# Seven experts of a mixture-of-experts layer, selected by one switch each instead of nested branches

## The chip, the core and the metric

The kernel runs on one core of a Trainium2 chip. A core has five engines with instruction streams of their own: TensorE (PE in the profile; its weight loads are listed as PEld), VectorE (DVE), ScalarE (ACT), GpSimd (POOL) and SyncE (SP), and 16 DMA engines that move data between memory and the core. The metric is device time in microseconds (us) of one execution; smaller is better.

## The reference

A block-sparse attention is followed by a mixture of experts in which some tokens skip the experts:

```python
def _attn_ref(q, k, v, sampled_blocks):      # B=4, H=8, S=768, D=64, blocks of 32
    scores = scale * np.matmul(q, k.transpose(0, 1, 3, 2))
    # kept: blocks next to each other, first and last block row and column, 3 sampled blocks a row
    scores = np.where(mask, scores, -1000000000.0)
    attn = softmax(scores)
    return np.matmul(attn, v)

def _moe_ref(x, w_skip, w_gate, w1, w2):     # x: 3072 tokens of 512; 8 experts, 1024 inner columns
    out = x.copy()
    xc = x[x @ w_skip > 0]
    e_idx = np.argmax(xc @ w_gate, axis=1)
    gate_w = softmax(xc @ w_gate)[row, e_idx]
    for e in range(E):
        h = np.maximum(xc[e_idx == e] @ w1[e], 0.0)
        y[e_idx == e] = gate_w[...] * (h @ w2[e])
    out[x @ w_skip > 0] = xc + y
    return out
```

How many tokens an expert gets is known only while the kernel runs. With these inputs the largest of the eight comes first; the sizes, in groups of 32 tokens, are 12 for expert 0 and then 8, 10, 9, 5, 2, 10 and 11 for experts 1 to 7, in the order in which the kernel works them off.

## The kernel before

The attention comes first (up to about 310 us): batch by batch, with the routing of finished tokens between its steps. It is not changed. The experts follow. Products are made in a split form: an operand is held as a high and a low part (`h` and `l` in the names), and each product is three matmuls, high by high, high by low, low by high.

Expert 0 has a branch of its own (`ahead`), in which counting, sorting and the first gathers stand between its matmuls. `counts()` makes `cnt`, the number of groups of 32 tokens of each expert, on VectorE; the sorted list `lt` follows it there, and GpSimd's gathers of token rows read that list.

Experts 1 to 7 stand one after the other in the program, each with the code for every size that it might have:

- `gemm1_any(n, e, x, each)` chooses a width by nested `tc.If` (lines 782 to 803) and calls `gemm1` (lines 746 to 754), 96 matmuls of 256 to 384 columns into PSUM tiles `hp`, which ScalarE and VectorE read as they come (`hh`, `hf`, `hl`); at most four groups go through `gemm1_tokens` (lines 768 to 778) instead.
- `outputs(p, n)` goes through the second product in chunks of 128 tokens. `last_chunk` (lines 898 to 914) does the last one first: whole (`gemm2`, lines 812 to 814), or, if it has only 64 or 32 tokens, by `gemm2_few` (line 824), chosen by two more compares; which chunk is the last is chosen by another two. In it the next expert's rows are turned (`turn`, line 588, PSUM tiles `tp` and `rps`). `full_chunks` (lines 934 and 938) does the others.
- Around these, weights are loaded two experts ahead (`load_w`, line 488: first weights on SyncE's queue, second ones on GpSimd's) and split into the two parts (`split_w`, lines 492 and 494). `close` (line 829) writes a chunk out, and `fetch_rows` (line 576) gathers rows for two experts ahead on GpSimd.

Each engine has its own instruction stream, and every engine runs every compare. An `If` of the program thus stands as compares and jumps in all five streams, and in each the code of the branches not taken lies between what is executed. The number `n` that the compares use is read by `tokens_of`:

```python
    n = tokens_of(1)
    for e in range(1, E):
        gemm1_any(n, e, x, parts(e))
        n = outputs(e, n)
```

The PSUM tiles come from pools: two tiles for turned rows (`ps_x`), three for the first product (`ps_h`), two for the second (`ps_y`), and the rest for the routing.

Of the kernel before, what the change touches and what calls it, by code (L numbers as in the profile page):

```python
# [30 lines left out]
CS = 3  # L31
# [3 lines left out]
NEVER = float(E * LC * P * P)  # L35
VA = 8
NEAR = 8
BATCHES = [[0, NB - 1, 1, 2], [3, 4, 5, 6], [7, 8, 9, 10], [11, 12, 13, 14], [15, 16, 17], [18, 19, 20], [21, 22]]


@with_exitstack
def tile_kernel(ctx, tc, qs, qd, kt, v, sb, wg, w1, w2, out):
# [548 lines left out]
    def keep_x(tps, xh, xl):  # L591
        for c, tp in enumerate(tps):
            cs = slice(P * c, P * c + P)
            nc.scalar.copy(out=xh[:, :, cs], in_=tp)
            nc.vector.tensor_tensor(out=xl[:, :, cs], in0=tp, in1=xh[:, :, cs].bitcast(F32), op=ALU.subtract)
# [115 lines left out]
    wp2 = ctx.enter_context(tc.tile_pool(name="wp2", bufs=1))  # L711
    mp = ctx.enter_context(tc.tile_pool(name="mp", bufs=2))
    mc = ctx.enter_context(tc.tile_pool(name="mc", bufs=1))
    ps_x = ctx.enter_context(tc.tile_pool(name="ps_x", bufs=2, space=PSUM))
    ps_h = ctx.enter_context(tc.tile_pool(name="ps_h", bufs=3, space=PSUM))
    ps_y = ctx.enter_context(tc.tile_pool(name="ps_y", bufs=2, space=PSUM))
    cnt = mc.tile([1, E], I32, name="cnt")
    mxc = mc.tile([1, 1], I32, name="mxc")
    one = mc.tile([1, 1], I32, name="one")
    lt = mc.tile([P, E * LC, 2], I32, name="lt")  # L720
    ends = mc.tile([P, CS, 2], I32, name="ends")
    lsw = mc.tile([P, LC, 2], I32, name="lsw")
# [113 lines left out]
    def counts():  # L836

        c = count("c")
        nc.vector.tensor_scalar(out=cnt, in0=c, scalar1=float(G - 1), scalar2=None, op0=ALU.add)
        nc.vector.tensor_single_scalar(out=cnt, in_=cnt, scalar=5, op=ALU.logical_shift_right)  # L840
        nc.vector.tensor_reduce(out=mxc, in_=cnt, axis=AX.X, op=ALU.max)
        er = nc.vector.value_load(perm[0:1, 0:1], min_val=0, max_val=E - 1)
        nc.vector.tensor_copy(out=one, in_=cnt[:, bass.ds(er, 1)])
        nc.vector.tensor_copy(out=cnt[:, bass.ds(er, 1)], in_=cnt[:, 0:1])
        nc.vector.tensor_copy(out=cnt[:, 0:1], in_=one)

    def lists():
        nc.sync.dma_start(out=lt, in_=lst3)
# [9 lines left out]
            gather(xs[p % 2][c], lt[:, p * LC + c, 0:1])  # L858

    def columns(xgs, x):  # L860
        keep_x(turn_x(xgs[:2], ps_x, "tp") + turn_x(xgs[2:], ps_r, "rps"), *x)

    def parts(p):

# [80 lines left out]
    def tokens_of(p):  # L945
        return nc.values_load(cnt[0:1, p:p + 1], min_val=0, max_val=N // G)

    def outputs(p, n):

        def split_next(zs):  # L950
            if p + 1 < E:
                for z in zs:
                    split_w("1", p + 1, z, 8, "hl", nc.gpsimd if z in (7,) else None)

        def turn():
            if p + 1 < E:
                columns(xs[(p + 1) % 2], x)

        last_chunk(p, n, lambda: split_next((0, 1)), turn)
        if p + 2 < E:  # L960
            load_w("1", p + 2)
        split_next(range(2, NEAR))
        nxt = tokens_of(p + 1) if 0 < p < E - 1 else None
        full_chunks(p, n)
        if p + 2 < E:
            load_w("2", p + 2, eng=nc.gpsimd)
        return nxt

    wt.update({"2" + t: wp2.tile([P, 4096], F32R, name=f"w2{t}") for t in "hl"})
    xs = [[mp.tile([P, DM], F32, name=f"x{z}{c}", bufs=1) for c in range(CS)] for z in range(2)]  # L970
# [7 lines left out]
    with tc.If(pv > 1) as ahead:  # L978
        px, p0, p1, d1, d2, rank, d3, d4 = last[0]()
        le = early["l"]  # L980
        load_w("2", 1, 0, 2)

        beside = [[px], [], [p0], [p1, d1], [d2], [], [], [rank, d3], [], [d4], [], [counts, lists, lambda: load_w("2", 1, 1, 2)]]
        splits = [[], [], [], [0], [1, 2], [3, 4], [5, 6], [7]]

        def go(n):
            for step in beside[n] if n < len(beside) else []:
                step() if callable(step) else run(step)

        for f in range(NK2):  # L990
            gemm1(0, early["t"], 256, None, [f], between=lambda: go(2 * f))
            go(2 * f + 1)
            for z in splits[f]:
                split_w("2", 0, z, 8)
        gemm2(0, 0, 0)
        order_lists()
        rows(0, [2])
        rows(1, range(CS))
        finish(0, early["x"][0], le.bitcast(F32)[:, 0, 1:2], le[:, 0, 0:1])
        clear()  # L1000
        gemm2(0, 1, 1, range(0, 6))
        keep_x(turn_x(xs[0][2:], ps_x, "tp"), *early["t"])
        gemm2(0, 1, 1, range(6, NK2))
        finish(1, early["x"][1], le.bitcast(F32)[:, 1, 1:2], le[:, 1, 0:1])
        n0 = tokens_of(0)
        with tc.If(n0 > 2 * CG):
            gemm1_tokens(0, early["t"])
        columns(xs[1], x)
        for z in range(NEAR):
            split_w("1", 1, z, 8)  # L1010
        load_w("1", 2)
        with tc.If(n0 > 2 * CG):
            gemm2(0, 0, 0)
            close(0, 2, 0, xs[0][2])
        rows(2, range(CS))
        load_w("2", 2, eng=nc.gpsimd)
# [13 lines left out]
        outputs(0, n0)  # L1030
    for z in range(2):
        nc.vector.tensor_scalar(out=ends[:, :, z], in0=lt[:, (E - 1) * LC:(E - 1) * LC + CS, 0], scalar1=2.0, scalar2=float(z), op0=ALU.mult, op1=ALU.add)
    n = tokens_of(1)
    for e in range(1, E):
        gemm1_any(n, e, x, parts(e))
        n = outputs(e, n)


    top = nc.values_load(mxc, min_val=0, max_val=N // G)
# [67 lines left out]
```

## Time and profile before

| what | value |
|---|---|
| time, median of 3 runs | 601.09 us (596.47 to 601.2) |
| the profiled execution | 606.04 us, its span 604.3 us |
| mean granted clock of TensorE | 0.925 |
| busy: TensorE, VectorE, ScalarE, GpSimd | 513.6, 369.8, 251.8, 216.6 us |
| experts 1 to 7 on TensorE | 361.9 to about 591 us |
| instruction transfers, queues q8 and q14 | 88 and 73 packets, 1.44 and 0.60 MB |

The profile is one execution. The chain of waits is followed back from the last instruction. A row of the timeline gives the start, the duration, engine, line, operation and tiles of an instruction (or of several alike, x4), and in brackets how long its engine was idle before it and what ended that, where "issue" stands for nothing that the profile shows. Branches and compares are not counted as busy and have no rows of their own. The granted clock is a share of full speed; 0.50 is half. A row of the DMA view gives a queue's packets, megabytes and share of the 16 engines in the window asked for; q8 and q14 carry instructions.

### The profile page before, as it was taken

To read this page: it belongs to the slowest core of one execution; us is meant where nothing else is said; L and a number is where in the kernel's file an instruction comes from. 1 tells how busy PE (TensorE), PEld (TensorE's weight loads), DVE (VectorE), ACT (ScalarE), POOL (GpSimd) and SP (SyncE) were. 2 spreads that over 40 slices of the span, in tenths; PEclk is the share of its full clock that TensorE was granted. 3 is DMA by queue.
4 is the path that set the end of the run, shared out by engine and by line. 5 is a ranking of instruction groups with operands and counts; after the bars stand their busy time and mean duration, and the time that the engine had idled before them with its cause. 6 is when DMAs were issued, how large, how long until landed. Compare 5 with 4: busy or idle time off the path is not lost.

```text
span 604.3 us, 16232 instructions
## 1 busy us (share of the span) xinstructions
PE 513.6 (85%) x5842; PEld 382.3 (63%) x5842; DVE 369.8 (61%) x1019; ACT 251.8 (42%) x576; POOL 216.6 (36%) x236
## 2 busy tenths in 40 slices
PE   7999999899898899996979768896887958859991
PEld 4777665466565465563668558694776946737981
DVE  4877578478577777787776066544466572735510
ACT  3444455355364355462733055343153535423500
POOL 2016363564655355646372321300404040602011
PEclk9999999799899699897988898987899888979997
DMA  9999899688799499788894415441625454630000
GB/s 295 342 299 236 190 259 243 153 219 211 174 215 232 115 227 224 167 229 214 247 322 142 172 27 179 172 180 24 218 108 178 152 189 158 214 125 26 19 33 22
DMA packets 49507, 108.03 MB, mean 179 GB/s; under 512 B 7175, under 2 KB 35208, under 8 KB 43842
## 3 DMA queue, kind: packets, MB, share of 16 engines
q1 hardware_dynamic: 43760, 84.69, 51.3%
q0 software_dynamic: 5008, 20.69, 9.7%
q8 instruction: 88, 1.44, 1.0%
q14 instruction: 73, 0.60, 0.3%
q10 hardware_dynamic: 578, 0.61, 0.3%
HBM read 96.34 MB, written 12.30 MB: 180 GB/s over the span
## 4 chain that ended last, share of the span: by engine, by line
PE 34%; issue 28%; DMA 21%; DVE 8%; POOL 3%; SPq 2%; POOLq 1%; ACT 0%; ACTq 0%; DVEq 0%
PE sp L400 11%; PE op L434 7%; PE tp L420 6%; DMA kts<-w 5%; DMA out<-o,lt 5%; DMA x<-out,lt 4%; DMA lst<-pay,adr 4%; PE op L356 4%; PE sp L321 3%; DVE m L409 3%; DVE m L408 3%; PE tp L344 2%; DMA out<-xs 2%; POOL out L72 1%; DVE xs L447 1%
## 5 line engine op out<-in xcount | busy, mean ns | idle before, releaser
L400 PE MATMUL sp<-kg,q 128*64 128x256 f32 x704 | 102.0, 408 | 2.8 <-issue 2.7
L424 ACT COPY pt<-tp 128x512 f32<-128x512 f32 x88 | 51.7, 588 | 108.1 <-PE tp L420 96.7
L408 DVE TENSOR_REDUCE m<-sp 128x2 f32<-128x512 f32 x88 | 60.2, 684 | 43.3 <-PE sp L400 35.5
L72 POOL DMA_INDIRECT out<-o,lt x17 | 19.4, 1139 | 179.2 <-DVE o L829 178.9
L201 POOL TENSOR_TENSOR kg<-kts,onesf 128x512 f32<-128x512 f32 x66 | 82.0, 1273 | 0.0
L415 ACT ACTIVATE pr<-sp,m 128x256 f32<-128x256 f32 x176 | 74.4, 478 | 8.0 <-DVE rs L445 8.0
L746 PE MATMUL hp<-xh,w1h 128*128 128x256 f32 (+3 forms) x192 | 61.3, 319 | 16.7 <-issue 8.3
L186 POOL TENSOR_SCALAR kg<-kts 128x512 f32<-128x512 f32 x50 | 30.1, 627 | 125.5 <-PE sp L400 87.4
L400 PEld LDWEIGHTS sp<-kg,q 128*64 128x64 f32 x704 | 45.2, 141 | 36.5 <-issue 24.5
L420 PE MATMUL tp<-ident,pr 128*128 128x128 f32 x352 | 61.8, 297 | 4.4 <-issue 4.4
L434 PEld LDWEIGHTS op<-va,pt 128*32 128x32 f32 x1376 | 31.9, 112 | 47.3 <-ACT pt L424 24.9
L747 PE MATMUL hp<-xl,w1h 128*128 128x256 f32 (+3 forms) x192 | 60.6, 316 | 0.0
L748 PE MATMUL hp<-xh,w1l 128*128 128x256 f32 (+3 forms) x192 | 60.5, 315 | 0.0
L751 ACT ACTIVATE hh<-hp 128x256 fp32r<-128x256 f32 (+2 forms) x56 | 21.2, 381 | 93.6 <-PE hp L748 51.6
L434 PE MATMUL op<-va,pt 128*32 128x65 f32 x1376 | 49.5, 232 | 11.3 <-DVE xs L447 8.5
L434 PE MATMUL op<-vb,pt 128*32 128x65 f32 x1376 | 50.6, 227 | 3.1 <-issue 2.9
L754 DVE SCALAR_TENSOR_TENSOR hl<-hp,hh 128x256 fp32r<-128x256 f32 (+2 forms) x56 | 23.4, 419 | 46.8 <-ACT hf L753 28.4
L746 PEld LDWEIGHTS hp<-xh,w1h 128*128 128x128 f32 x192 | 39.1, 204 | 19.1 <-issue 19.1
L420 PEld LDWEIGHTS tp<-ident,pr 128*128 128x128 f32 x352 | 38.9, 145 | 14.2 <-issue 6.9
L812 PE MATMUL yp<-w2h,hh 128*128 128x512 f32 x112 | 45.0, 402 | 2.7 <-ACT w1h L492 1.6
L813 PE MATMUL yp<-w2l,hh 128*128 128x512 f32 x112 | 44.1, 394 | 0.3 <-DVE o L829 0.3
L814 PE MATMUL yp<-w2h,hl 128*128 128x512 f32 x112 | 44.2, 394 | 0.0
(207 smaller groups left out, 1013.2 us busy)
## 6 DMA issues: line engine op xcount, KB each, us to landing
vb<-v SPq DMA_DIRECT2D x68, 260.0 KB
va<-v SPq DMA_DIRECT2D x48, 260.0 KB
kts<-w SPq DMA_DIRECT2D x6, 2048.0 KB
kts<-w POOLq DMA_DIRECT2D x6, 2048.0 KB
q<-qs SPq DMA_DIRECT2D x22, 512.0 KB
vt<-v SPq DMA_DIRECT2D x16, 390.0 KB
kts<-w SPq DMA_DIRECT2D x12, 512.0 KB
kts<-kt SPq DMA_DIRECT2D x15, 384.0 KB
```

The source lines that it names most:

```text
L201: nc.gpsimd.tensor_tensor(out=kg[x][:, :, c0:c0 + BS], in0=kts[:, :, bass.ds(kr * BS, BS)], in1=onesf[:, 0:BS].unsqueeze(1).broadcast_to([ ...
L400: nc.tensor.matmul(out=self.sp[64 * j:64 * j + 64, g, :], lhsT=qt[self.i][:, p, :], rhs=kg[self.x][:, p, :], start=True, stop=True)
L408: lambda: nc.vector.reduce_max(out=self.mx, in_=self.sp, axis=AX.X),
L415: nc.scalar.activation(out=self.pr[:, g, :], in_=self.sp[:, g, :], func=AF.Exp, bias=self.mx[:, g:g + 1], scale=SCALE)
L420: nc.tensor.transpose(out=self.tp[:, u, :], in_=self.pr[:, u // 2, (u % 2) * P:(u % 2) * P + P], identity=ident)
L424: nc.scalar.copy(out=self.pt, in_=self.tp)
L434: nc.tensor.matmul(out=self.op[32 * hh:32 * hh + 32, g, :], lhsT=self.pt[:, 2 * g + t, 32 * hh:32 * hh + 32], rhs=vt[:, 8 * self.b + 4 * g ...
L746: nc.tensor.matmul(out=hp[:, 0:w], lhsT=wh[:, f, k, :], rhs=xh[:, k, 0:w], start=(k == 0), stop=False)
L747: nc.tensor.matmul(out=hp[:, 0:w], lhsT=wh[:, f, k, :], rhs=xl[:, k, 0:w], start=False, stop=False)
L748: nc.tensor.matmul(out=hp[:, 0:w], lhsT=wl[:, f, k, :], rhs=xh[:, k, 0:w], start=False, stop=(k == NK1 - 1))
L812: nc.tensor.matmul(out=yp, lhsT=hh[:, f, cs], rhs=wh[:, f, :], start=(f == 0), stop=False)
L814: nc.tensor.matmul(out=yp, lhsT=hl[:, f, cs], rhs=wh[:, f, :], start=False, stop=(f == NK2 - 1))
```

## The change

One `tc.Switch` per expert takes the place of all compares between the first product and the end of the second. It has ten arms, for n = 1, 2, 4, 5, 6, 8, 9, 10, 11 and 12 groups (`KINDS`); each arm is a whole expert, `expert(p, n)`, written with n as a constant, so that nothing in an arm branches. Sizes between two kinds take the next larger arm.

- `counts()` makes `kinds` on VectorE: for each expert the number of kinds that `cnt` exceeds, one instruction and then eight more. `kind_of` reads an entry, one expert ahead.
- The PSUM pools `ps_x` (2) and `ps_h` (3) become one pool `ps_h` of five; turned rows take `hp` tiles from it. In expert 0's branch, too, they do.
- The gathers for the chunks from the last one upwards now stand together behind the last chunk. For five groups `gemm1` writes 160 columns, where the old code wrote 192; the matmuls are 256 wide in both.

```diff
-    ps_x = ctx.enter_context(tc.tile_pool(name="ps_x", bufs=2, space=PSUM))
-    ps_h = ctx.enter_context(tc.tile_pool(name="ps_h", bufs=3, space=PSUM))
+    ps_h = ctx.enter_context(tc.tile_pool(name="ps_h", bufs=5, space=PSUM))
...
         nc.vector.tensor_copy(out=cnt[:, 0:1], in_=one)
+        nc.vector.tensor_scalar(out=kinds, in0=cnt, scalar1=float(KINDS[0]), scalar2=None, op0=ALU.is_gt)
+        for n in KINDS[1:-1]:
+            nc.vector.scalar_tensor_tensor(out=kinds, in0=cnt, scalar=float(n), in1=kinds, op0=ALU.is_gt, op1=ALU.add)
...
     def columns(xgs, x):
-        keep_x(turn_x(xgs[:2], ps_x, "tp") + turn_x(xgs[2:], ps_r, "rps"), *x)
+        keep_x(turn_x(xgs[:2], ps_h, "hp") + turn_x(xgs[2:], ps_r, "rps"), *x)
...
+    def kind_of(p):
+        return nc.values_load(kinds[0:1, p:p + 1], min_val=0, max_val=len(KINDS) - 1)
+
+    def expert(p, n):
+
+        if n > CG:
+            gemm1(p, x, G * n, parts(p), few=G * (n % CG) if n % CG < 3 else 0)
+        else:
+            gemm1_tokens(p, x)
+            if n > 2:
+                for f in range(NK2):
+                    split_w("2", p, f, 8)
...
+        c = (n - 1) // CG
+        if c == 0:
+            turn()
+        split_next((0, 1))
+        m = G * (n - CG * c)
+        if m > 64:
+            gemm2(p, c, 1)
+            close(p, c, 1, xs[p % 2][c])
+        else:
+            gemm2_few(p, c, m, 1)
+            close(p, c, 1, xs[p % 2][c], m)
+        if c:
+            turn()
+        for y in range(c, CS):
+            fetch_rows(p + 2, y)
+        if p + 2 < E:
+            load_w("1", p + 2)
+        split_next(range(2, NEAR))
+        for y in range(c):
+            if p == E - 1 and y == c - 1:
+                halves(p, y, y)
+            else:
+                gemm2(p, y, y)
+                close(p, y, y, xs[p % 2][y])
+                fetch_rows(p + 2, y)
+        if p + 2 < E:
+            load_w("2", p + 2, eng=nc.gpsimd)
...
-    n = tokens_of(1)
+    nxt = kind_of(1)
     for e in range(1, E):
-        gemm1_any(n, e, x, parts(e))
-        n = outputs(e, n)
+        kind, nxt = nxt, kind_of(e + 1) if e + 1 < E else None
+        for z in tc.Switch(kind, len(KINDS), hint=f"expert{e}"):
+            expert(e, KINDS[z])
```

Three places show how instructions move. The rows are in the order of the program, with the code of all branches or arms; `hp`, `yp` are PSUM tiles of the first and the second product, `kts` the loaded weights, `w2h` and `w2l` their split parts.

First TensorE's stream where expert 1 ends and expert 2 begins, before:

```order
L814 MATMUL yp_6625<-w2h,hl 128x512
L938 UNCONDITIONAL_BRANCH x2
L782 COMPARE_AND_BRANCH
L783 COMPARE_AND_BRANCH
L784 COMPARE_AND_BRANCH
L746 MATMUL hp<-xh,w1h 128x384
```

and after:

```order
L815 MATMUL yp_6624<-w2h,hl 128x512
L1148 UNCONDITIONAL_BRANCH
L972 TENSOR_LOAD kinds
L1148 SWITCH_STRIDE
L1148 ISA x2
L1088 BRANCH_PREFETCH_HINT
L769 MATMUL hp<-w1h,xh 128x512
```

The three compares ahead of the first matmul are gone (three or four are executed, by size); in their place stand the read of the table, a register operation and an indirect jump (the two rows marked ISA). The hint that opens each arm names the place at which the arm will leave the switch.

Second, TensorE's stream around the last chunk of expert 2 when that chunk is the third, before:

```order
L814 MATMUL yp_6626<-w2h,hl 128x512
L898 UNCONDITIONAL_BRANCH
L902 COMPARE_AND_BRANCH
L824 MATMUL yp_6626<-kts,hf 64x512 x8
L902 UNCONDITIONAL_BRANCH
L824 MATMUL yp_6626<-kts,hf 32x512 x8
L902 UNCONDITIONAL_BRANCH
L588 MATMUL tp<-ident,x_6614 128x128 x4
```

and after, in the arm for ten groups:

```order
L749 MATMUL hp<-xh,w1l 128x320
L825 MATMUL yp_6624<-kts,hf 64x512 x8
L589 MATMUL hp<-ident,x_6612 128x128 x4
L589 MATMUL hp<-ident,x_6613 128x128 x4
L589 MATMUL rps<-ident,x_6614 128x128 x4
L813 MATMUL yp_6623<-w2h,hh 128x512
```

The few-row products follow the first product directly, and the next expert's rows are turned into `hp` tiles.

Third, VectorE's stream in expert 0's branch, where the counts are made, before:

```order
L843 COPY one<-cnt 1x1
L844 ISA
L844 COPY cnt<-cnt 1x1
L845 COPY cnt<-one 1x1
L494 TENSOR_TENSOR w2l<-kts,w2h 128x512 x2
```

and after:

```order
L845 ISA
L845 COPY cnt<-cnt 1x1
L846 COPY cnt<-one 1x1
L847 TENSOR_SCALAR kinds<-cnt 1x8
L849 SCALAR_TENSOR_TENSOR kinds<-cnt,kinds 1x8 x8
L495 TENSOR_TENSOR w2l<-kts,w2h 128x512 x2
```

Nine instructions on 8 numbers stand ahead of the rest of the second weights' split and of the sorted list.

More of the change, by code (lines that the diff above doesn't have):

```diff
@@ L37 @@
 NEAR = 8
+KINDS = [1, 2, 4, 5, 6, 8, 9, 10, 11, 12]
 BATCHES = [[0, NB - 1, 1, 2], [3, 4, 5, 6], [7, 8, 9, 10], [11, 12, 13, 14], [15, 16, 17], [18, 19, 20], [21, 22]]
@@ L719, in tile_kernel @@
     one = mc.tile([1, 1], I32, name="one")
+    kinds = mc.tile([1, E], I32, name="kinds")
     lt = mc.tile([P, E * LC, 2], I32, name="lt")
@@ L962, in outputs @@
         split_next(range(2, NEAR))
-        nxt = tokens_of(p + 1) if 0 < p < E - 1 else None
         full_chunks(p, n)
@@ L966, in outputs, with split_next, turn @@
             load_w("2", p + 2, eng=nc.gpsimd)
-        return nxt
+    def kind_of(p):
[8 more added lines that the diff above has]
+                    split_w("2", p, f, 8)
+        def split_next(zs):
+            if p + 1 < E:
+                for z in zs:
+                    split_w("1", p + 1, z, 8, "hl", nc.gpsimd if z in (7,) else None)
+        def turn():
+            if p + 1 < E:
+                columns(xs[(p + 1) % 2], x)
+        c = (n - 1) // CG
[25 more added lines that the diff above has]
+            load_w("2", p + 2, eng=nc.gpsimd)
     wt.update({"2" + t: wp2.tile([P, 4096], F32R, name=f"w2{t}") for t in "hl"})
@@ L1001, in tile_kernel @@
         gemm2(0, 1, 1, range(0, 6))
-        keep_x(turn_x(xs[0][2:], ps_x, "tp"), *early["t"])
+        keep_x(turn_x(xs[0][2:], ps_h, "hp"), *early["t"])
         gemm2(0, 1, 1, range(6, NK2))
```

## The prediction

> **What bounds the kernel now.** I read the page first: the shares of the engines and the chain that ended last.
>
> ```profile
> span 604.3 us, 16232 instructions
> PE 513.6 (85%) x5842; PEld 382.3 (63%) x5842; DVE 369.8 (61%) x1019; ACT 251.8 (42%) x576; POOL 216.6 (36%) x236
> PE 34%; issue 28%; DMA 21%; DVE 8%; POOL 3%; SPq 2%; POOLq 1%; ACT 0%; ACTq 0%; DVEq 0%
> ```
>
> TensorE is busy 85% of the time, but 28% of the chain is "issue": the engine waits for nothing that the profile shows. The change touches experts 1 to 7, which TensorE works on from 361.9 us to about 591 us. The busy time by stretch, here for that whole part and for experts 2, 5 and 7 (columns: window, its length, busy TensorE, weight loads, VectorE, ScalarE, GpSimd, then the granted clock, the DMA share and GB/s):
>
> ```profile
> 355.00:592.00 237.00, 193.23 (x1079) 165.64 (x1077) 122.65 (x193) 84.44 (x203) 52.45 (x48) 0.91 0.36 128
> 390.00:431.00 41.00, 33.50 (x170) 28.32 (x171) 19.15 (x31) 13.76 (x35) 9.40 (x9) 0.88 0.42 153
> 491.00:515.00 24.00, 14.63 (x60) 10.43 (x60) 8.68 (x14) 8.51 (x17) 4.44 (x5) 0.79 0.41 143
> 554.00:592.00 38.00, 36.19 (x209) 33.22 (x207) 12.73 (x21) 7.76 (x16) 4.88 (x5) 1.00 0.09 32
> ```
>
> TensorE is idle 44 of 237 us; VectorE works 123 of them and DMA is busy 36%, so neither can be the limit over the stage. Expert 7, the last, shows what an undisturbed one looks like: 36 of 38 us busy at full clock. The waits of TensorE from 355 to 592 us (total, times, longest) put names to the idle time:
>
> ```profile
> PE yp L824 <- issue: 11.7, 2, 7.1
> PE hp L746 <- issue: 8.3, 3, 3.1
> PE hp L768 <- issue: 7.3, 1, 7.3
> PE hp L746 <- DVE ends L1032: 5.3, 1, 5.3
> PE hp L746 <- DVE w1l L494: 3.0, 1, 3.0
> PE yp L824 <- DVE w2l L494: 2.0, 1, 2.0
> PE yp L812 <- ACT w1h L492: 1.6, 1, 1.6
> PE yp L824 <- ACT w1h L492: 1.5, 1, 1.5
> PE yp L812 <- DVE hl L754: 1.1, 1, 1.1
> ```
>
> Together 41.8 us. Every one stands where the program branches: L746 and L768 open the first product of an expert, behind the compares of `gemm1_any`; L824 and L812 open the last chunk, behind those of `last_chunk`. The timeline gives the places (start, duration, operation, in brackets the idle time before):
>
> ```profile
> 392.87 0.39 PE L746 MATMUL hp<-xh,w1h 128*128 128x320 f32 x1 [3.06 <-issue]
> 413.36 2.79 PE L824 MATMUL yp<-kts,hf 128*64 128x512 f32 x5 [4.63 <-issue]
> 434.03 0.37 PE L746 MATMUL hp<-xh,w1h 128*128 128x288 f32 x1 [2.36 <-issue]
> 468.29 0.36 PE L746 MATMUL hp<-xh,w1h 128*128 128x256 f32 x1 [2.89 <-issue]
> 497.78 0.77 PE L768 MATMUL hp<-w1h,xh 128*128 128x512 f32 x1 [7.30 <-issue]
> 539.25 3.77 PE L824 MATMUL yp<-kts,hf 128*64 128x512 f32 x8 [7.10 <-issue]
> ```
>
> What is waited for in such a gap the DMA view tells. First the queue of instruction transfers in 532.0 to 539.2 us, the gap ahead of the 7.10; then the same queue in 427.8 to 428.2 us; last, TensorE from 427.90 to 431.60 us:
>
> ```profile
> q8 instruction: 2, 0.03, 2.0%
> ...
> q8 instruction: 1, 0.02, 13.9%
> ...
> 427.90:431.60 3.70, 3.70 (x17) 2.81 (x15) 0.00 (x0) 0.00 (x0) 2.04 (x2) 1.00 0.40 125
> ```
>
> Two fetches of 16 KB of instructions fill the idle 7.10 us, at most 3.55 us each. The third row says what hides a fetch: the one at 428 us, for expert 3's entry, began 3.7 us before TensorE ran out of matmuls. The idle time there was 2.36, so two fetches in series took 3.7 + 2.36 = 6.1 us, 3.0 each. A hop thus costs 3.0 to 3.55 us; one alone hides behind the queued 512-wide products, two in a row do not.
>
> The idle time has a second price, the clock. Stretches at half clock after the gaps, and one after the 3.01 us gap that kept full clock:
>
> ```profile
> 360.00:366.60 6.60, 4.73 (x22) 4.76 (x23) 1.57 (x4) 0.89 (x2) 3.66 (x4) 0.50 0.71 186
> 393.97:397.35 3.38, 3.38 (x15) 3.38 (x14) 1.12 (x2) 1.00 (x3) 0.57 (x1) 0.50 0.82 246
> 414.00:417.80 3.80, 3.80 (x11) 1.82 (x9) 0.00 (x0) 0.00 (x0) 0.00 (x0) 0.50 0.00 0
> 434.95:438.30 3.35, 3.35 (x16) 3.35 (x16) 1.10 (x2) 0.98 (x3) 0.72 (x2) 0.50 0.69 187
> 469.10:472.40 3.30, 3.30 (x18) 3.30 (x17) 0.98 (x2) 0.90 (x3) 0.32 (x1) 0.50 0.70 194
> 492.90:503.10 10.20, 5.32 (x13) 4.24 (x14) 2.23 (x4) 0.00 (x0) 2.70 (x4) 0.50 0.54 163
> 537.35:544.10 6.75, 4.85 (x12) 2.17 (x14) 0.00 (x0) 0.00 (x0) 0.00 (x0) 0.50 0.02 5
> 517.90:524.00 6.10, 6.10 (x42) 6.10 (x43) 5.01 (x7) 2.62 (x9) 5.61 (x4) 1.00 0.77 307
> ```
>
> Work at half clock takes twice its time, so half of the busy 28.7 us in the first seven rows, 14.4 us, is lost. Idle and clock together: 56.2 us.
>
> **The change part by part.** *Branches inside an expert.* An arm holds the whole expert as straight code, so the waits ahead of L824 and L812 go: 11.7 + 2.0 + 1.6 + 1.5 + 1.1 = 17.9 us. Some bear an operand's name (w1h, w2l, hl), not "issue"; I take them for fetches too, since the operands named were made on engines that run the same compares.
>
> *Branches at an entry.* Expert 1's 5.3 follows the code ahead of the loop and stays. The others are 8.3 + 7.3 + 3.0 = 18.6 us now, with none at expert 7. In place of three or four compares stand one read of the table of kinds and one indirect jump. The way out of an arm is announced at its start by a hint; the way in is not, so one hop remains, 3.0 to 3.55 us against the 3.7 that run ahead: 0 if it hides, about 3 if the run-ahead is lost (the lone gaps of 2.4 to 3.1). No row prices the table read. I take 1 us for each of experts 2, 3, 4, 6 and 7, nearer to zero because the run-ahead was measured. Expert 5's 7.30 fell among weight loads and was two hops: (7.30 + 3.7) / 2 = 5.5 for one, 1.8 beyond the run-ahead, with the table read 2.5. Entries after: 5 + 2.5 = 7.5, a gain of 11.1 us.
>
> *Clock.* With gaps of 1 us, the half-clock rows at 393.97, 414.00, 434.95, 469.10 and 537.35 go: (3.38 + 3.80 + 3.35 + 3.30 + 4.85) / 2 = 9.3 us. Those at 360 and 492.9 I leave. The rows do not give a sure bound: gaps of 2.36 were followed by half clock, the one of 3.01 was not. [...]
>
> *The table of kinds.* `counts()` gets nine small VectorE instructions. The rows, with the work behind them and the chain they stand in:
>
> ```profile
> 323.11 0.14 DVE L839 TENSOR_SCALAR cnt<-rps 1x8 int32<-1x8 f32 x1
> 323.29 0.16 DVE L840 TENSOR_SCALAR cnt<-cnt 1x8 int32<-1x8 int32 x1
> 324.65 0.14 DVE L845 COPY cnt<-one 1x1 int32<-1x1 int32 x1
> 329.82 1.04 POOL L576 DMA_INDIRECT x<-out,lt  x1 [5.82 <-DVE lt L854]
> 339.16 0.34 PE L588 MATMUL tp<-ident,x 128*128 128x128 f32 x1 [4.14 <-DMA x<-out,lt]
> ```
>
> From start to start 0.18 us, so 9 x 0.18 = 1.6 us. Behind them VectorE still owes the sorted list `lt`, on which GpSimd's gather waits, and on the gather TensorE (4.14 us). Between 0, if the gather's landing is set elsewhere, and 1.6; I take 1.0. The instructions are added on that path, so a gain is excluded.
>
> *Five PSUM tiles.* No wait in the list above names `hp` or `tp` as not free, so five shared tiles gain 0. A turned row now takes a tile of the first product; it comes after that product was read, in expert 5 right behind it, where a sixth tile waits for the first one's reader: 0 to the 1.5 us that the last chunk there waits for ScalarE now (L824, w1h), taken 0.
>
> *Order of gathers, 160 instead of 192 columns.* In a two-chunk expert one gather, in expert 5 three, now come ahead of GpSimd's share of the next split: 1.04 us each, so 1 to 3 us late for a slice that is the last of eight to be used. Taken 0, at most 3 if that slice ends last. The number of matmuls stays. In expert 4 ScalarE and VectorE read 32 columns less in eight tiles, off the path: 0.
>
> Sum: 17.9 + 11.1 + 9.3 - 1.0 = 37.3 us. The profiled execution took 606.04 us (span 604.3, the rest around it) and would take 568.7; it lies 5 us above the median of 601.09, so from the median 563.8, **564 us**.
>
> **The rivals.** *Operands end last.* Once the fetches are gone the waits named w1h, w2l, hl and w1l stay, because VectorE and ScalarE are late themselves: 2.0 + 1.6 + 1.5 + 1.1 + 3.0 = 9.2 us less gain, of which 1 for expert 6's entry is already counted: 8, 572 us. For it speaks the row at 517.90, with VectorE busy 5.01 of 6.10 us; against it 123 of 237 over the stage.
>
> *One hop uncovered at every entry.* The sequencer reaches the jump too late: six entries at 3 us are 18, so of 18.6 only 0.6 is gained; of the clock only the mid-expert stretches, (3.80 + 4.85) / 2 = 4.3, less 0.8 for a new one now and then at expert 7. 17.9 + 0.6 + 4.3 - 0.8 - 1.0 = 21.0: 580 us. For it: the lone entry gaps of 2.36 to 3.06; against it: two hops, not one, explain that of 2.36.
>
> *Two hops in series per expert.* An arm is longer than one block of code, so the jump out is fetched as well as the jump in. Five entries at 3.2 and expert 5 at 7.3 make 23.3, 4.7 more than now: 17.9 - 4.7 + 4.3 - 0.8 - 1.0 = 15.7, 585 us. [...]
>
> *Slower: entries that cost what expert 5's does.* Bigger code between targets, beside the weight loads, makes each of seven entries 7.30 idle plus 5.32 / 2 = 2.7 of clock: 70 us against 56.2 now, with the table 1 more: 601.09 + 14.8 = 616 us. It turns from gain to loss at (56.2 - 1.0) / 7 = 7.9 us an entry. For it: 7.30 did occur; against it: it occurred once, and with two hops.
>
> **How the numbers follow.** About 1%, 6 us, is what a measurement of this kernel tells from no change. Chances: the forecast 0.47 (558 to 569), operands 0.14 (572), one hop 0.12 (580), two hops 0.11 (585), slower 0.07 (616); 0.05 for two hops with arms that also stall once inside, 595 to 607 (585 and another 1.5 to 3 us in each of seven experts); 0.04 below 558, if every entry hides its hop (564 less 7.5 is 556). The range, 555 to 589, reaches from that last case over both hop cases, with 4 us for the gathers and tiles taken at 0, and leaves out the slower one and the stalling arms. Faster by over 1% (below 595): 0.47 + 0.14 + 0.12 + 0.11 + 0.04 = 0.88; within 1%: 0.05; slower: 0.07.
>
> **What would show it.** Right: no idle time ahead of the few-row products and of the second product's first matmul in any of experts 2 to 7; one gap of 0 to 1.5 us at each entry, one fetch in it; the clock from 390 us on 0.97 or more but for expert 5; TensorE's busy share in this part above 0.92 in place of 193 / 237 = 0.82. The table: VectorE's list copies some 1.6 us later behind the counts. Wrong: entry gaps of 3 us or more (a hop uncovered) or with two fetches; gaps that wait for w1l, w2l or hl in mid-expert (operands).

## The result, and the profile after

The changed kernel takes 581.08 us in the median of four runs (573.99 to 582.86), against 601.14 us before: a ratio of 0.958, with a 95% interval of 0.951 to 0.965. The forecast was 564 us with a range of 555 to 589. Timed once more in six runs, the changed kernel took 576.54 us, ratio 0.962 (0.957 to 0.967). The ratios leave out the runs that were taken as slow, so they are not the quotients of the medians (0.967 and 0.960). The gain is 23 to 25 us by these ratios and 20 and 24 us by the medians, where 37.3 had been worked out.

The profiled execution took 573.99 us. Of its page, the span, the chain that ended last, and the queues that carry instructions:

```profile
span 572.3 us, 16047 instructions
PE 43%; issue 27%; DVE 12%; DMA 8%; POOL 4%; SPq 1%; POOLq 1%; ACT 1%; DVEq 0%; ACTq 0%
q8 instruction: 70, 1.15, 1.0%
q14 instruction: 149, 1.22, 0.7%
```

Of the two queues of code, q8, whose packets fall in TensorE's gaps, has 70 packets where there were 88; q14 has 149 where there were 73. Without any switches (below) they have 51 and 43. I take q8 for TensorE's fetches, a block of 16 KB a packet (1.15 MB in 70), and q14 for the other engines': the first have become fewer, the second have doubled.

The two executions differ by 32.0 us of span. To see where, I cut the span at two instructions of TensorE's timeline: the first matmul of expert 1, and the last matmul of expert 7. The first had stood at 361.87 us; the last, of the timeline before:

```profile
591.05 0.28 PE L885 MATMUL yp<-w2h,hl 128*128 128x256 f32 x1
```

Both, in the timeline after:

```profile
356.61 0.55 PE L747 MATMUL hp<-xh,w1h 128*128 128x256 f32 x1 [5.01 <-issue]
555.36 0.27 PE L889 MATMUL yp<-w2h,hl 128*128 128x256 f32 x1
```

Before, the experts' span was 591.33 - 361.87 = 229.5 us; now it is 555.63 - 356.61 = 199.0 us, 30.4 us less. The part ahead of it, attention and expert 0, ended 5.3 us earlier, and the part behind it grew from 13.0 to 16.7 us. 30.4 + 5.3 - 3.7 = 32.0.

The 5.3 us are not the change's. Expert 0's first matmul, ahead of which the attention is unchanged, stands at 307.03 us before and at 301.25 after, 5.8 us earlier; from there to expert 1 it is 54.8 us and 55.4. In the thirteen profiles of this study the first matmul of expert 1 lies anywhere from 350.5 to 363.0 us. The granted clock of that part differs too, 0.94 and 0.97.

What the change did is thus 30.4 - 3.7 = 26.7 us in this pair of profiles. The second profile of the changed kernel has 229.5 - 201.2 = 28.2 us less in the experts and 3.8 us more behind them, 24.4. Both are near the 23 to 25 of the ratios, and the total time of a single run says little about it. The experiments below are therefore read by the experts' span, and by the gaps within it.

TensorE's waits in that part of the changed kernel, the gaps at the entries of experts 2, 5 and 6, and four windows (the whole part; experts 2, 5, 6):

```profile
PE hp L747 <- DVE o L830: 7.5, 5, 2.0
PE hp L747 <- issue: 5.0, 1, 5.0
PE hp L769 <- DVE o L830: 4.2, 1, 4.2
PE hp L589 <- issue: 2.4, 1, 2.4
PE hp L747 <- DVE hl L755: 2.0, 1, 2.0
PE hp L776 <- ACT h L772: 0.3, 1, 0.3
```

```profile
383.74 0.39 PE L747 MATMUL hp<-xh,w1h 128*128 128x320 f32 x1 [1.62 <-DVE o L830]
469.24 0.76 PE L769 MATMUL hp<-w1h,xh 128*128 128x512 f32 x1 [4.19 <-DVE o L830]
487.18 0.39 PE L747 MATMUL hp<-xh,w1h 128*128 128x320 f32 x1 [1.95 <-DVE o L830]
```

```profile
356.00:556.00 200.00, 182.62 (x1072) 155.53 (x1072) 112.25 (x185) 82.46 (x200) 49.02 (x47) 0.97 0.44 152
381.00:412.00 31.00, 29.38 (x168) 24.41 (x167) 19.52 (x31) 13.75 (x35) 8.57 (x9) 1.00 0.46 164
463.00:484.00 21.00, 14.15 (x65) 9.87 (x65) 10.17 (x15) 6.31 (x14) 6.29 (x7) 0.92 0.56 191
484.00:520.00 36.00, 32.02 (x172) 26.10 (x169) 22.17 (x37) 15.85 (x40) 11.58 (x9) 0.95 0.45 154
```

The waits ahead of L824 and L812 are gone from the list. TensorE is busy 183 of 200 us, 0.91, where it was 0.82, and expert 2 runs at full clock. Six entry gaps are left (the five of 7.5 us together, and 4.2): 11.7 us. Two gaps stand where there were none of that size: 2.4 us inside expert 5 (L589) and 2.0 us inside expert 6 (L747, "DVE hl").

### The profile page after: what moved, and what is told of

It reads as the page before. It is cut to its first block, busy times and chain, and to the rows that moved or that the text cites. A ratio compares the mean times of both kernels' runs of the same rounds, so it can differ in the third digit from the quotient of the medians.

```text
span 572.3 us, 16047 instructions
## 1 busy us (share of the span) xinstructions
PE 499.7 (87%) x5842; PEld 369.4 (65%) x5842; DVE 358.0 (63%) x1028; ACT 250.8 (44%) x576; POOL 214.8 (38%) x236
## 3 DMA queue, kind: packets, MB, share of 16 engines
q8 instruction: 70, 1.15, 1.0%
## 4 chain that ended last, share of the span: by engine, by line
PE 43%; issue 27%; DVE 12%; DMA 8%; POOL 4%; SPq 1%; POOLq 1%; ACT 1%; DVEq 0%; ACTq 0%
PE sp L401 11%; PE op L435 7%; PE tp L421 7%; DMA x<-out,lt 6%; PE op L357 4%; PE sp L322 3%; DVE m L409 3%; DVE m L410 2%; PE tp L345 2%; POOL out L73 2%; POOL x L577 2%; DVE xs L448 1%; PE hp L749 1%; PE hp L747 1%; DMA kts<-kt 1%
## 5 line engine op out<-in xcount | busy, mean ns | idle before, releaser
L401 PE MATMUL sp<-kg,q 128*64 128x256 f32 x704 | 100.5, 405 | 1.6 <-issue 1.6
L747 PE MATMUL hp<-xh,w1h 128*128 128x256 f32 (+3 forms) x192 | 59.5, 310 | 14.6 <-DVE o L830 7.5
L421 PE MATMUL tp<-ident,pr 128*128 128x128 f32 x352 | 60.4, 292 | 4.2 <-issue 4.1
L748 PE MATMUL hp<-xl,w1h 128*128 128x256 f32 (+3 forms) x192 | 58.9, 307 | 0.0
L749 PE MATMUL hp<-xh,w1l 128*128 128x256 f32 (+3 forms) x192 | 58.8, 306 | 0.0
L435 PE MATMUL op<-va,pt 128*32 128x65 f32 x1376 | 48.3, 228 | 7.5 <-issue 2.2
L435 PE MATMUL op<-vb,pt 128*32 128x65 f32 x1376 | 49.0, 223 | 6.6 <-issue 6.6
L747 PEld LDWEIGHTS hp<-xh,w1h 128*128 128x128 f32 x192 | 37.3, 194 | 17.7 <-issue 15.4
L421 PEld LDWEIGHTS tp<-ident,pr 128*128 128x128 f32 x352 | 38.1, 143 | 12.8 <-issue 5.0
```

Source lines behind the costliest of these rows:

```text
L401: nc.tensor.matmul(out=self.sp[64 * j:64 * j + 64, g, :], lhsT=qt[self.i][:, p, :], rhs=kg[self.x][:, p, :], start=True, stop=True)
L421: nc.tensor.transpose(out=self.tp[:, u, :], in_=self.pr[:, u // 2, (u % 2) * P:(u % 2) * P + P], identity=ident)
L435: nc.tensor.matmul(out=self.op[32 * hh:32 * hh + 32, g, :], lhsT=self.pt[:, 2 * g + t, 32 * hh:32 * hh + 32], rhs=vt[:, 8 * self.b + 4 * g ...
L747: nc.tensor.matmul(out=hp[:, 0:w], lhsT=wh[:, f, k, :], rhs=xh[:, k, 0:w], start=(k == 0), stop=False)
L748: nc.tensor.matmul(out=hp[:, 0:w], lhsT=wh[:, f, k, :], rhs=xl[:, k, 0:w], start=False, stop=False)
L749: nc.tensor.matmul(out=hp[:, 0:w], lhsT=wl[:, f, k, :], rhs=xh[:, k, 0:w], start=False, stop=(k == NK1 - 1))
```

## The experiments

All spans here are the experts' span, in us, with the idle time of TensorE in it (gaps over 0.2 us), from the timelines.

| kernel | span | idle |
|---|---|---|
| before | 229.5 | 37.8 |
| after | 199.0 | 16.4 |
| after once more | 201.2 | 14.8 |
| sizes fixed, no switches | 179.4 | 2.1 |
| six arms | 202.1 | 16.2 |
| no arm for twelve | 203.1 | 17.4 |
| two switches per expert | 237.2 | 43.0 |
| after with the old pools, two profiles | 211.5, 212.6 | 23.7, 24.8 |
| before with the pool of five | 230.4 | 38.1 |
| without expert 6's first weights | 200.3 | 16.5 |
| next switch announced | 204.2 | 17.4 |
| expert 1's arm announced | 203.9 | 16.9 |

Each span is one profile. The two of the changed kernel differ by 2.2 us, and two edits that were meant to leave the experts alone (no arm for twelve, expert 1's arm announced) gave 203.1 and 203.9. Differences of less than some 4 us therefore say nothing here.

**Are the gaps jumps?** The profile names VectorE's closing of a chunk for the entry gaps. The first experiment takes the switches out:

```diff
-    nxt = kind_of(1)
     for e in range(1, E):
-        kind, nxt = nxt, kind_of(e + 1) if e + 1 < E else None
-        for z in tc.Switch(kind, len(KINDS), hint=f"expert{e}"):
-            expert(e, KINDS[z])
+        expert(e, (0, 8, 10, 9, 5, 2, 10, 11)[e])
```

> The changed kernel without its seven switches: each expert is straight code for the size that it has with these inputs (8, 10, 9, 5, 2, 10, 11 groups), so the choice by count is left out. Measure: the experts' span, from the first matmul of expert 1 to the last of expert 7, 229.5 us before and 199.0 us after the change. Theory (instruction fetches): the gaps that are left at the entries of experts 2 to 7 (11.7 us together), the 2.0 us inside expert 6 and the half clock behind the longer ones (about 3 us) are all the price of the jumps, on TensorE or on the engines that feed it: the span falls to 180 to 184 us. Rival (operands): the profile names VectorE's closing of a chunk and its split for those gaps; if it is right they stay, and the span is 195 to 199 us.

The span was 179.4 us, a little below what I expected, and the time 544.52 us (ratio 0.910, 0.903 to 0.917). All waits of TensorE there:

```profile
PE hp L589 <- DMA x<-out,lt: 1.4, 1, 1.4
PE hp L770 <- DVE w1l L495: 0.4, 1, 0.4
PE hp L776 <- ACT h L772: 0.3, 1, 0.3
```

The same part as a window:

```profile
355.00:534.00 179.00, 176.92 (x1073) 151.66 (x1071) 118.50 (x190) 82.87 (x200) 52.26 (x48) 1.00 0.45 165
```

VectorE, ScalarE and the loads do the same work, and every entry gap is gone; TensorE is busy 176.9 of 179 us at full clock. So the operands that the profile named were not what was waited for at the entries, and what the seven switches still cost within this span is 199.0 - 179.4 = 19.6 us: 14.3 of idle time (16.4 - 2.1), the other 5.3 of busy time, which half clock lengthens (the granted clock of the part was 0.97 with the switches and is 1.00 without; in the changed kernel's expert 6 the products of 320 columns start 0.15 us apart at full clock and 0.27 apart at half, 1.8 times). Outside of it, expert 1's entry gap of 5.0 us is gone too, and the part behind the experts is 12.8 us, where the changed kernel has 16.7.

**Does the distance or the number of arms matter?**

```diff
-KINDS = [1, 2, 4, 5, 6, 8, 9, 10, 11, 12]
+KINDS = [2, 5, 8, 9, 10, 11]
```

> The changed kernel with only the six arms that these inputs use (2, 5, 8, 9, 10, 11 groups; other sizes are left out), so that the jumps are shorter and the program smaller. Theory: a jump costs its fetch whatever its distance; entry gaps of 1.2 to 2.0 us and one of about 4 us stay, span 199 us plus or minus 2. Rival (size of the code between targets decides): the gaps shrink, span 193 us or less.

It was 202.1 us, 1.1 more than I expected, with entry gaps of 1.40, 1.21, 1.82, 2.21, 2.27 and 1.10 and gaps of 3.63 and 2.33 us inside experts 5 and 6. Fewer arms and a smaller program thus earned nothing. But the 4 us at expert 5 did not come: from the start of the jump's packet of q8 to the first matmul it took 2.8 us with one packet (462.36 to 465.14), where the changed kernel has two packets and 4.6 us (464.68 to 469.24). The arm for two groups is the first of the switch here. So the jump to a near target was cheaper here, by 1.8 us; this was seen once.

**Does a jump in mid-expert cost as much?**

```diff
-    def expert(p, n):
+    def first_product(p, n):
...
+    def expert(p, n):
...
+        for z in tc.Switch(kind, len(KINDS), hint=f"first{e}"):
+            first_product(e, KINDS[z])
         for z in tc.Switch(kind, len(KINDS), hint=f"expert{e}"):
             expert(e, KINDS[z])
```

> The changed kernel with two switches per expert on the same kind, one around the first product and one around the rest: seven more jumps, in mid-expert. Theory: a jump takes about 4.1 us, the sequencer is some 2 us ahead at the end of a first product, so about 2 us idle each, with half clock behind some: the experts' span grows from 199 to 213 to 225 us. Rival (jumps are nearly free, the gain of the change came from elsewhere): 205 us or less.

It was 237.2 us, in this one profile more than the 229.5 of the nested compares, and outside of what I expected on the upper side. TensorE's waits:

```profile
PE hp L747 <- issue: 13.8, 6, 4.7
PE yp L825 <- issue: 12.7, 4, 4.7
PE hp L589 <- issue: 10.9, 1, 10.9
PE yp L813 <- issue: 6.0, 2, 3.2
PE hp L769 <- issue: 4.0, 1, 4.0
```

Six of the seven new jumps show ahead of the second product, 12.7 + 6.0 = 18.7 us: about 3 each, 4.7 in one case, more than the 2 that I had put down. The seventh is the 10.9 us in expert 5, whose second arm begins with the turned rows (L589); that size I had not expected. Three packets of q8 fall in it, one and then two for the jump. Of the 38.2 us that the span grew, 26.6 are idle time (43.0 - 16.4); the rest is busy time, in an execution with a mean granted clock of 0.924 where the changed kernel's had 0.96. From a jump's first packet of q8 to the first instruction behind it, the six took 4.3 to 4.5 us, and the six entries of the changed kernel 4.4 to 4.7. So the jump takes the same at both places, and what it leaves idle depends on how long TensorE still has matmuls when it begins: 1.2 to 2.0 us are left behind a full chunk (4.2 at expert 5), about 3 behind a first product.

**What did the pool do?** The forecast gave it nothing. First the changed kernel with the old pools (the edit below), then the kernel before with the new pool (the same edit the other way round):

```diff
-    ps_h = ctx.enter_context(tc.tile_pool(name="ps_h", bufs=5, space=PSUM))
+    ps_x = ctx.enter_context(tc.tile_pool(name="ps_x", bufs=2, space=PSUM))
+    ps_h = ctx.enter_context(tc.tile_pool(name="ps_h", bufs=3, space=PSUM))
...
-        keep_x(turn_x(xgs[:2], ps_h, "hp") + turn_x(xgs[2:], ps_r, "rps"), *x)
+        keep_x(turn_x(xgs[:2], ps_x, "tp") + turn_x(xgs[2:], ps_r, "rps"), *x)
...
```

> The changed kernel with the two PSUM pools of before (two tiles for turned rows, three for the first product). Theory: five shared tiles earn nothing, since the gain is the branches': the experts' span stays at 199 us, plus or minus 2. Rival (the pool earned part of it): TensorE waits for a tile of the first product, and the span is 204 us or more.

> The kernel before with the pool of five alone, nested compares kept. Theory: experts' span 229 us, plus or minus 3, with the same gaps at the same places. Rival (the pool earned part of it): 224 us or less.

Alone the pool earns nothing: 230.4 us against 229.5. Beside the switches it does: 211.5 us without it, 12.5 more than with it. My theory failed on the first of the two. The kernel with the old pools was then timed:

> The kernel with the switches and the two old PSUM pools once more, now timed: its first look had an experts' span of 211.5 us against 199.0 with the pool of five, against the theory that the pool earns nothing. New theory: VectorE and ScalarE make jumps of their own and enter an arm late; five tiles let TensorE run on for five slices of the first product meanwhile, three tiles for three. Then the waits for VectorE inside the first products of experts 3, 4 and 6 come again, 7 to 10 us together, span 208 to 214 us, and the time lies 1.5 to 2.5% above the changed kernel's. Rival (chance): span 199 to 203.

It took 590.7 us, ratio 0.984 (0.969 to 0.999), against 0.958 and 0.962 for the changed kernel, and the span was 212.6 us: with two profiles of each kernel, the old pools cost 10.3 to 13.6 us of span. The waits of TensorE for VectorE inside the first products, in the first profile with the old pools:

```profile
PE hp L748 <- DVE hl L756: 9.0, 3, 5.5
```

And in the second:

```profile
PE hp L748 <- DVE hl L756: 9.8, 3, 6.1
```

The timelines at expert 6 show what is behind them. First the kernel with the old pools, where TensorE begins at 489.34, stops and goes on at 500.36, and VectorE's first instruction of that arm is at 499.88:

```profile
489.34 0.39 PE L748 MATMUL hp<-xh,w1h 128*128 128x320 f32 x1 [2.24 <-DVE w1l L495]
499.88 0.42 DVE L756 SCALAR_TENSOR_TENSOR hl<-hp,hh 128x256 fp32r<-128x256 f32 x1 [8.19 <-issue]
500.36 0.63 PE L748 MATMUL hp<-xh,w1h 128*128 128x320 f32 x1 [5.49 <-DVE hl L756]
```

Then the changed kernel, where TensorE had begun at 487.18; the first instructions of ScalarE and VectorE in the arm, and TensorE's second start:

```profile
493.18 0.38 ACT L752 ACTIVATE hh<-hp 128x256 fp32r<-128x256 f32 x1 [6.68 <-issue]
497.77 0.42 DVE L755 SCALAR_TENSOR_TENSOR hl<-hp,hh 128x256 fp32r<-128x256 f32 x1 [7.96 <-ACT hf L754]
498.25 0.42 PE L747 MATMUL hp<-xh,w1h 128*128 128x320 f32 x1 [2.03 <-DVE hl L755]
```

In both, VectorE comes into the arm 10.5 to 10.6 us after TensorE (499.88 - 489.34; 497.77 - 487.18), after 8 us of idle time; ScalarE is late here too, by 6 us. They have jumps of their own to make: without switches VectorE comes 4.7 us after TensorE at this place, and works until then. Meanwhile TensorE fills as many tiles as there are: it stopped after 498.25 - 2.03 - 487.18 = 9.04 us with five, and after 500.36 - 5.49 - 489.34 = 5.53 us with three, 1.8 us a tile. Two more tiles thus cover 3.5 us of VectorE's lateness here, and all of it in experts 3 and 4, where the old pools have gaps of 1.8 and 1.7 us. Of the 12.5 us, 7.3 are idle time (23.7 - 16.4); the other 5.2 are busy time, which half clock behind the gaps can lengthen; against the second profile of the changed kernel the busy time differs by only 1.4.

Why the pool earns nothing alone shows in the kernel before, where TensorE begins expert 3 at 434.03:

```profile
437.12 0.42 DVE L754 SCALAR_TENSOR_TENSOR hl<-hp,hh 128x256 fp32r<-128x256 f32 x1 [4.65 <-ACT hf L753]
```

VectorE comes 3.1 us after TensorE there, and 2.6 to 3.3 us at experts 2, 4, 6 and 7. With the old pools and the switches three tiles lasted 4.6 us at expert 4 and 5.5 us at expert 6, so before the change no product ran out of them. With one switch per expert VectorE comes 5.6 to 6.4 us after TensorE at experts 2, 3, 4 and 7, and 10.6 at expert 6.

**Why is expert 5's entry longer than the others?**

> The changed kernel without the transfer of expert 6's first weights (left out, so its products are of old data); in the changed kernel these 2 MB move while TensorE waits at expert 5's entry. Theory: that entry's 4.2 us, against 1.2 to 2.0 at the others, is the same jump with its fetch slowed by the transfer: it falls to 1.2 to 2.0 us, the experts' span from 199 to 195 to 197 us. Rival (expert 4's short last chunk or the small arm makes it long): the entry stays above 3.5 us.

The entry gap fell from 4.19 to 1.43 us, as the first theory had it; but the span stayed, 200.3 us, which neither had, and the trace does not bear out the theory's mechanism. The queue q8 from the start of the jump's first packet to the first matmul of expert 5, in the changed kernel (464.6 to 469.2 us) and without the load (468.5 to 473.2); then the stretch ahead of that, again in both (458.1 to 464.6, and 465.3 to 468.5):

```profile
q8 instruction: 2, 0.03, 3.6%
q8 instruction: 2, 0.03, 4.1%
q8 instruction: 1, 0.02, 0.8%
q8 instruction: 1, 0.02, 1.7%
```

The jump itself is no slower beside the load: 4.6 us from its first packet to the first matmul (464.68 to 469.24), 4.7 without the load (468.55 to 473.25). What differs is when it begins: 0.4 us before TensorE runs out of matmuls, or 3.3. The packet ahead, in the middle of expert 4's arm, starts at 458.15 beside the load, which was issued at 458.20, and 6.5 us pass until the jump's; without the load 3.2 us pass (465.33 to 468.55). In the second profile of the changed kernel it is 6.8 us, with a gap of 4.32. So the load delays a block of code ahead of the jump, and with it the jump. The entry without the load, and a gap further on in the same expert:

```profile
473.25 0.47 PE L770 MATMUL hp<-w1h,xh 128*128 128x512 f32 x1 [1.43 <-DVE w1l L496]
487.00 0.45 PE L590 MATMUL hp<-ident,x 128*128 128x128 f32 x1 [5.09 <-issue]
```

The queue of GpSimd's transfers in the DMA view from 480.4 to 487.0 us, around that gap:

```profile
q0 software_dynamic: 139, 1.95, 72.9%
```

Expert 6's second weights, 2 MB on GpSimd's queue, issued at 478.50, move while TensorE stands in the middle of straight code, waiting for nothing that is named. The gap is ahead of the second tile of turned rows, as the 2.4 us of the changed kernel are; without switches the second tile follows the first without a gap. Whether it is a block of code that is fetched slowly beside the transfer is not shown: one packet of q8 falls in the changed kernel's gap (478.2 to 480.6 us), none in this one.

**Can the jump be announced?** Chunk 0 of experts 1 to 6 was moved behind the switch, with a hint for the next arm ahead of it:

```diff
...
         for z in tc.Switch(kind, len(KINDS), hint=f"expert{e}"):
             expert(e, KINDS[z])
+        if e < E - 1:
+            tc.switch_hint({g: nxt for g in GS}, len(KINDS), f"expert{e + 1}")
+            gemm2(e, 0, 0)
+            close(e, 0, 0, xs[e % 2][0])
...
```

> The changed kernel with the next switch announced: for experts 1 to 6 the full chunk 0 (24 matmuls of the second product, its closing, one gather, one weight load) is taken out of the arms and stands behind the switch, and ahead of it each engine gives a hint that names the next expert's arm. A size of at most four groups does chunk 0 whole here and splits all its second weights (expert 5: some 2 to 4 us more work). Theory (what is left at the entries is one jump with its fetch, on TensorE and on the engines that feed it): entry gaps of experts 2 to 7 fall from 11.7 us to 3 or less, the gap inside expert 6 goes, the experts' span falls from 199 to 184 to 190 us. Rival (a hint of 5.5 us of TensorE work ahead comes too late, or is lost): span 199 to 203 us with entry gaps as before.

The span was 204.2 us, the time 581.71 us (ratio 0.969, 0.957 to 0.981): nothing gained. Four of the gaps, the first and third ahead of chunk 0, the others at entries:

```profile
378.16 0.47 PE L813 MATMUL yp<-w2h,hh 128*128 128x512 f32 x1 [1.64 <-ACT w1h L493]
385.84 0.39 PE L747 MATMUL hp<-xh,w1h 128*128 128x320 f32 x1 [1.85 <-issue]
436.13 0.80 PE L813 MATMUL yp<-w2h,hh 128*128 128x512 f32 x1 [2.68 <-DVE o L830]
494.78 0.60 PE L747 MATMUL hp<-xh,w1h 128*128 128x320 f32 x1 [6.59 <-issue]
```

The entries of experts 4 and 7 lost their gaps, that of expert 3 shrank to 0.38; but now the ways out of three arms show gaps (1.64, 2.68 and 1.80), and expert 6's entry grew to 6.59. Yet the hint shows at five of the six entries: there the jump has one packet of q8 in place of two, and 1.3 to 3.1 us pass from its start to the first matmul; only expert 5's entry has two, and 4.5 us. At expert 6 the one packet starts 3.9 us after TensorE ran out of matmuls (488.19 to 492.12). Why so late, and why ways out that had no gap now have one, stays open. A hint for expert 1 alone, well ahead in expert 0's branch, was tried beside the changed kernel:

```diff
         load_w("1", 2)
+        early_kind = kind_of(1)
+        tc.switch_hint({g: early_kind for g in GS}, len(KINDS), "expert1")
         with tc.If(n0 > 2 * CG):
...
```

> The changed kernel with one addition: in expert 0's branch, ahead of its last 24 matmuls, every engine gives a hint that names expert 1's arm. Theory (expert 1's entry gap of 5.0 us is the way out of that branch and then the jump with its fetch; a hint 5 us ahead takes the second): the gap falls to 0.5 to 3 us, a gain of 2 to 5 us with half clock of up to 2 us behind it gone. Rival (a hint so early is lost, as it was at four of the six entries in the kernel with hints): gap 4.6 to 5.1 us as in all runs so far, time unchanged.

> The changed kernel once more, unchanged, timed in more rounds. Its first profile has expert 1's first matmul at 356.6 us; other runs with the same code ahead of that matmul have it anywhere from 350.5 to 362 us. Theory (the gain of the change is 30 us in the experts and the rest of the difference between two executions is the unchanged part's): the experts' span comes again at 196 to 203 us, the entry gaps at 1.2 to 2.0 us with one of 2 to 4.5 at expert 5, and the median is 18 to 30 us below the kernel before. Rival (the first profile was lucky in the experts): span 204 us or more.

In the profiled execution with the hint (581.18 us, the longest of its six) the gap was 3.53 us, between what the two had:

```profile
359.26 0.36 PE L747 MATMUL hp<-xh,w1h 128*128 128x256 f32 x1 [3.53 <-issue]
```

The other profiles with switches have 4.7 to 5.3 us there. With the hint two packets of q8 lie between 352.5 us and this matmul; the changed kernel's second profile has three on the same way, from 345.8 us. So the hint took one fetch away. The times were 574.56 us (ratio 0.955, 0.950 to 0.961) with the hint and 576.54 us (0.962, 0.957 to 0.967) without: the intervals overlap, so this is at most a small gain and not a shown one. The changed kernel's span came again at 201.2 us.

**Where do 3.7 us at the end come from?** GpSimd's last scatter starts 12.2 us from the end of the span before, and 15.9 us after. The arm for eleven groups, which expert 7 takes, has one arm behind it:

```diff
-KINDS = [1, 2, 4, 5, 6, 8, 9, 10, 11, 12]
+KINDS = [1, 2, 4, 5, 6, 8, 9, 10, 11]
```

> The changed kernel without the arm for twelve groups, so that the arm that expert 7 takes (eleven groups) is the last of its switch (a size of twelve is left out). From the start of GpSimd's last scatter to the end of the span it was 12.2 us before the change, 15.9 after it, 12.9 with six arms (eleven last), 12.0 without switches. Theory: the 3.7 us are the way out of expert 7's arm on VectorE and GpSimd, a jump past the arm for twelve that has to fetch its target; with nothing to jump past, 12.0 to 13.0 us. Rival (a fixed price of a switch with many arms): 15.5 to 16.5 us. The experts' span stays at 196 to 204 us by both.

The last scatter before, where the span was 604.3 us:

```profile
592.13 0.97 POOL L72 DMA_INDIRECT out<-o,ends  x1 [1.90 <-DVE o L886]
```

After, where it was 572.3:

```profile
556.43 0.97 POOL L73 DMA_INDIRECT out<-o,ends  x1 [1.86 <-DVE o L890]
```

And without the arm for twelve, where it was 573.8:

```profile
560.95 0.97 POOL L73 DMA_INDIRECT out<-o,ends  x1 [1.86 <-DVE o L890]
```

573.8 - 560.95 = 12.9 us, as with six arms (12.9); the eight profiles with an arm for twelve have 15.6 to 16.1. With no arm to jump past, 3.0 of the 3.7 us are gone: the way out cost them, in spite of the hint at the arm's start. On which engine it did, and where the other 0.7 come from, stays open.

## Why the prediction was right, and where its sum was not

The direction, the range and the cause held: the idle time was jumps, and taking the jumps out of an expert takes their gaps away. The size did not: the medians of 581 and 577 us lie outside the 558 to 569 that the forecast itself was given, and within the range because it was drawn over the rivals. In the profiled pair the sum had 38.3 us for the experts (17.9 + 11.1 + 9.3), and 30.4 were measured (28.2 with the second profile). By its own steps:

- *Branches inside an expert, 17.9 us.* All the waits of the list went, those with an operand's name too, so reading w1h, w2l and hl as fetches was right. The kernel before had shown it: each of the gaps from expert 1's last chunk on, whatever it is put down to, ends 2.5 to 3.3 us after a packet of q8 starts (without the three of under 0.7 us inside experts 4 and 5). But the arm is not free of gaps: 2.41 us in expert 5 and 2.03 us in expert 6 came, 4.4 us, which the step did not have. The second is VectorE's late entry, and a wait for hl in mid-expert was the prediction's own sign for the rival of late operands. The step that failed is the silence on the other engines: it priced the jumps of TensorE alone, though each of the engines makes them.
- *Entries, 18.6 to 7.5 us.* Measured 11.7 (1.62, 1.32, 1.24, 4.19, 1.95, 1.38). That a jump is what is left was right; its size was off, by 4.2 us, and so was the sign of "one fetch in it". The step had one hop of 3.0 to 3.55 us, from pairs of jumps before, against 3.7 us that run ahead. At all six entries there are two packets of q8, the second 0.7 to 1.5 us behind the first, and 4.4 to 4.7 us from the first one to the first matmul; TensorE still had 2.5 to 3.4 us of matmuls then, and 0.4 at expert 5. So both the price of a jump and the run-ahead were mis-sized, and three of the six gaps are over 1.5 us. Expert 5's is not a slower jump, as the step had it, but a lost run-ahead. The queue q8 in the window from 439.6 to 444.4 us of the changed kernel, around the entry of expert 4:

```profile
q8 instruction: 2, 0.03, 3.9%
```

- *Clock, 9.3 us.* The experts' span fell by 30.4 us and its idle time by 21.4, so 9.0 us came from the clock, granted at 0.91 before and 0.97 after. In the second profile the clock gave 28.2 - 23.0 = 5.2 us, so that the size was met in the first is luck. The step took work at half clock for twice as long; by the 1.8 times that expert 6 shows, its five rows cost 8.4 us, not 9.3. With gaps of 1.2 to 1.6 us expert 2 ran at 1.00, experts 5 and 6 at 0.92 and 0.95 (0.97 or more had been the sign for all but expert 5). TensorE's busy share was 0.91, where above 0.92 had been the sign.
- *Expert 1's entry, left at 5.3:* 5.0.
- *The table of kinds, 1.0 us.* VectorE takes 1.6 us more, as the upper end had it; what it costs TensorE is less. The rows are the count's first instruction, the table, the first gather and the turned row that waits for it:

```profile
316.66 0.14 DVE L840 TENSOR_SCALAR cnt<-rps 1x8 int32<-1x8 f32 x1
318.38 0.16 DVE L847 TENSOR_SCALAR kinds<-cnt 1x8 int32<-1x8 int32 x1
318.58 1.48 DVE L849 SCALAR_TENSOR_TENSOR kinds<-cnt,kinds 1x8 int32<-1x8 int32 x8
325.10 1.03 POOL L577 DMA_INDIRECT x<-out,lt  x1 [7.15 <-DVE lt L858]
332.93 1.11 PE L589 MATMUL hp<-ident,x 128*128 128x128 f32 x4 [4.20 <-DMA x<-out,lt]
```

From the count to the gather it is 8.4 us where it was 6.7; from the count to the turned row 16.3 where it was 16.1. The landing took up 1.5 us, in this pair of executions.

- *Five PSUM tiles, 0.* This was wrong as a term of this change, by 10.3 to 13.6 us, though true of the pool by itself. The argument read the waits of before, where no product waited for a tile. It missed that with the switches VectorE comes into an expert later, and that the tiles decide how long TensorE goes on alone. Without the pool the sum would have been off by far more. That two omissions, the other engines' jumps and the tiles that cover most of them, offset each other was luck.
- *Order of gathers, 160 columns, 0.* These were not tried alone; no wait in the changed kernel's list names a gather.
- *The end, not in the sum:* 3.7 us more.

38.3 - 4.4 - 4.2 leaves 29.7 of the 30.4 measured; the rest is small gaps and the clock. Of the rivals, "one hop uncovered at every entry" gave 580 us and so comes close to the median, but not by its mechanism: its gaps of 3 us were seen at one entry of six. A part of its loss of clock gain, 9.3 to 3.5 us, was seen in the second profile (5.2). "Two hops in series" had the two fetches right, but the second starts 0.7 to 1.5 us behind the first, not a whole hop, and its entries of 3.2 us did not come. "Operands end last" is refuted for the entries by the kernel without switches; inside expert 6 TensorE did wait for VectorE, which was late because of its jump. The slower case, 7.9 us and more an entry, did not come about; with twice the jumps, however, the switches lose to the compares.

## What to carry to other kernels

The jumps on runtime values were paid here on more engines than TensorE: with one switch VectorE came into expert 6's arm 10.6 us after TensorE, and 4.7 us after it without. So when one engine's gap is taken away, look at which engine comes into the arm last, and whether there are buffers enough for the others to go on meanwhile. An edit that earns nothing by itself can be what makes another one pay, so a zero read from the waits of before holds only as long as the order of arrival does. And where the part that is not changed varies by more than the effect, measure the effect between two instructions of the trace.

## What was not expected of the hardware

A wait that the profile puts down to an operand (VectorE's closing, 11.7 us in six gaps) was a jump in all six: all of it went with the switches, at the same work. An announced jump was not always a cheap one: the way out of expert 7's arm cost 3.0 us, and of the six announced entries two were free while one took 6.6 us. A weight load of 2 MB delayed a block of straight code and not the jump behind it: 6.5 us passed from that block's fetch to the next, against 3.2 without the load, and the jump that came late left TensorE idle for 4.2 us. And straight code stood still for 5.1 us beside a transfer that held 73% of the DMA engines' time.
